# Unread matmuls ahead of the first batch's kv: six of them made to wait for a cast of k

## The chip, the cores and the metric

One core of a Trainium2 chip. The metric is the time of one execution on the device, in microseconds (us), as the median of several; differences here are tenths of a microsecond of 288, so single executions are listed where they matter. The profile's span, from the first to the last instruction, is a different clock: in the runs below the time is the span plus 1.8 to 1.9 us.

## The reference

Linear attention, then layer norm and a two-layer feed-forward, on 8 batches of 8 heads, 576 positions and 64 per head:

```python
kv  = einsum('bhsd,bhse->bhde', k, v)
o   = einsum('bhsd,bhde->bhse', q, kv)
x   = o / sqrt(mean(o*o, -1) + 1e-6) * g_norm          # then heads side by side: (8, 576, 512)
xn  = (x - mean) / sqrt(var + 1e-6) * g_ln
out = x + relu(xn @ w_ch1) @ w_ch2                     # 512 -> 2048 -> 512
```

## The kernel before

Almost all of the time is large matrix products on PE (TensorE). The argument is about the first 17 us, in which batch 0 is loaded, its kv is formed and a first tile is taken to the first large product. All loads of v, q and the weights come through POOL's queue, in this order; k comes as float32 by two other queues and is cast by DVE and ACT:

```python
nc.sync.dma_start(k_f[:, :HP // 2], pairs(k, 0, HP // 2))
nc.scalar.dma_start(k_f[:, HP // 2:], pairs(k, HP // 2, HP))
nc.gpsimd.dma_start(v_p[:, :HP - 1], pairs(v, 0, HP - 1))          # three of four pairs of heads: "v"
nc.gpsimd.dma_start(q_in[0][:64, :, :2], lo(q, 0)[:, :, :2])
nc.gpsimd.dma_start(v_p[:, HP - 1:], pairs(v, HP - 1, HP))
nc.gpsimd.dma_start(q_in[0][:64, :, 2:], lo(q, 0)[:, :, 2:])
load_w1(0)
# ...
nc.vector.tensor_copy(k_p[:, :HP // 2], k_f[:, :HP // 2])
nc.scalar.copy(k_p[:, HP // 2:], k_f[:, HP // 2:])
```

While these run PE has nothing to do, and is kept busy with products of zeros that nobody reads ("fills"). More of them stand between later steps of the start:

```python
def fill(n, p1=None):
    if p1 is None:
        p1 = ps2.tile([128, 512], f32, tag="p2", name="p1")
    for _ in range(n):
        nc.tensor.matmul(p1, lhsT=fill_sb[:, :128], rhs=fill_sb, start=True, stop=True)
    return p1
# ...
fill(18)
# ...
kv_a.mms()            # 54 products of 64x64 for three pairs; waits for k's cast and for v
kv_a.copies()
turn_first(0, ps2, "p2")
kv_a.times_g()
fill(1)
kv_b.mms()            # the fourth pair
# ... o, squares, sums, root, a scaled copy, then the large products
```

## Time and profile before

| | |
|---|---|
| median of three timed runs | 288.02 us (287.99 to 288.05) |
| the profiled run | 290.37 us, span 288.5 us, mean clock 0.993 |
| PE busy | 280.6 us, 97% of the span |
| fills end, then kv starts | 6.93 us, 9.51 us |
| first large product starts | 17.09 us |

In a timeline line the first number is the start, the second the length, and the bracket says how long the engine had been idle and what released it. In a line of windows, the numbers after the length are the busy time of PE, of its weight loads, of DVE, ACT and POOL, each with a count of instructions; then come the granted clock of PE (1.00 is full speed), the share of the DMA engines, and GB/s. The lines of this profile stand in the prediction.

### The profile page before, as it was taken

How to read it: one execution, taken by the hardware profiler on the slowest of the kernel's cores; microseconds unless marked ns; L12 is line 12 of the kernel's file. 1: busy time of each engine (PE TensorE's matmuls, PEld its weight loads, DVE VectorE, ACT ScalarE, POOL GpSimd, SP SyncE). 2: the span in 40 equal slices, each digit the busy share in tenths (PEclk: the TensorE clock that was granted, in tenths of full speed). 3: DMA queues.
4: the chain of work that ended last, by engine and by line, in shares of the span. 5: the costliest groups of instructions: out<-in, count | busy, mean ns of one | idle time of the engine just before them, and what ended most of it. 6: DMA issues, size and time to landing. Idle time of an engine off the chain costs nothing.

```text
span 288.5 us, 5777 instructions
## 1 busy us (share of the span) xinstructions
PE 280.6 (97%) x2302; PEld 159.2 (55%) x2302; DVE 150.4 (52%) x335; ACT 152.9 (53%) x334; POOL 44.2 (15%) x74
## 2 busy tenths in 40 slices
PE   7699999999999999999999999999999999999995
PEld 3479855996569644445444544444444444444444
DVE  5566207946997884675366565762578200220022
ACT  3367754796649733882289248920894076016500
POOL 8432630023025004100620020000000000000000
PEclk9799999999999999999999999999999999999999
DMA  7999999949988989994999897038202610131033
GB/s 207 199 205 204 199 183 190 228 94 172 149 164 131 187 134 176 212 133 97 155 221 190 144 128 163 18 63 173 58 18 60 106 36 0 41 83 24 0 74 73
DMA packets 67442, 36.76 MB, mean 127 GB/s; under 512 B 35536, under 2 KB 62548, under 8 KB 67416
## 3 DMA queue, kind: packets, MB, share of 16 engines
q0 software_dynamic: 28736, 18.29, 44.4%
q1 hardware_dynamic: 38168, 17.39, 31.3%
q10 hardware_dynamic: 512, 0.72, 0.8%
q8 instruction: 18, 0.29, 0.4%
q14 instruction: 8, 0.07, 0.1%
HBM read 36.71 MB, written 9.44 MB: 160 GB/s over the span
## 4 chain that ended last, share of the span: by engine, by line
PE 94%; DMA 3%; ACT 1%; issue 0%; DVE 0%; POOLq 0%
PE p L489 43%; PE p L473 43%; DMA v_in<-in_v_dram 3%; PE o_ps L281 3%; PE kv_ps L254 2%; PE p L206 1%; PE tp L192 1%; ACT m L476 1%; PE og_ps L293 0%; ACT xT_blk L410 0%; PE odd L233 0%; PE tp L408 0%; ACT xT_blk L334 0%; DVE ss L358 0%; PE o_part L566 0%
## 5 line engine op out<-in xcount | busy, mean ns | idle before, releaser
L473 PE MATMUL p<-xT_blk,w_sb 128*128 128x128 bf16 (+2 forms) x1024 | 132.0, 286 | 0.6 <-ACT xT_blk L334 0.3
L489 PE MATMUL p<-w_sb,m 128*128 128x512 bf16 (+2 forms) x608 | 128.2, 368 | 0.0
L476 ACT ACTIVATE m<-p 128x512 bf16<-128x512 f32 x144 | 85.2, 595 | 46.8 <-PE p L473 44.5
L473 PEld LDWEIGHTS <-w_sb 128*128 128x128 bf16 x1024 | 78.6, 98 | 44.7 <-issue 1.3
L489 PEld LDWEIGHTS <-m 128*128 128x128 bf16 x608 | 57.3, 98 | 63.0
L494 DVE SCALAR_TENSOR_TENSOR o_sb<-p,rstd,x_blk 128x512 f32<-128x512 f32 (+2 forms) x38 | 27.2, 720 | 47.7 <-PE p L489 47.5
L287 ACT ACTIVATE sq<-o_ps 128x512 f32<-128x512 f32 x35 | 20.9, 596 | 27.0 <-PE o_ps L281 26.8
L400 ACT ACTIVATE dev<-x_blk,st_blk 128x512 f32<-128x512 f32 x36 | 25.7, 714 | 13.1 <-DVE st_blk L386 13.1
L358 DVE TENSOR_REDUCE ss<-sq 128x8 f32<-128x512 f32 x35 | 23.6, 678 | 16.4 <-ACT sq L287 16.4
L392 DVE SCALAR_TENSOR_TENSOR xc<-x_blk,st_blk,g_ln_sb 128x512 bf16<-128x512 f32 x34 | 25.6, 752 | 1.5 <-DVE st_blk L386 0.3
L363 DVE TENSOR_TENSOR y<-o_ps,inv 128x512 f32<-128x512 f32 x33 | 22.8, 692 | 3.1
L382 DVE SCALAR_TENSOR_TENSOR x_blk<-y,g_norm_sb 128x512 f32<-128x512 f32 x33 | 22.8, 692 | 1.1
L375 DVE RECIPROCAL inv<-rms 128x8 f32<-128x8 f32 x36 | 7.2, 201 | 22.9 <-ACT rms L368 22.9
L482 DVE RECIPROCAL rstd<-rstd 128x4 f32<-128x4 f32 x9 | 1.6, 174 | 30.8 <-ACT rstd L481 30.7
L368 ACT ACTIVATE rms<-ss,eps_sb 128x8 f32<-128x8 f32 x36 | 10.6, 295 | 11.6 <-DVE ss L358 11.5
L281 PEld LDWEIGHTS <-qt 128*128 128x128 bf16 (+1 forms) x156 | 10.6, 102 | 6.3 <-issue 0.7
L281 PE MATMUL o_ps<-kv_pack,qt 128*128 128x128 bf16 (+1 forms) x156 | 13.8, 221 | 0.0
L98 POOL COPY gate<-qt 1x1 bf16<-1x1 bf16 x5 | 0.9, 176 | 82.1 <-DMA qt<-q_p 82.1
L206 PE MATMUL p<-fill_sb 128*128 128x512 bf16 x24 | 8.2, 489 | 1.3 <-DVE eps_sb L142 1.3
L259 ACT CAST kv_pack<-kv_ps 64x256 bf16<-64x256 f32 x7 | 2.6, 365 | 11.4 <-PE kv_ps L254 11.4
L400 ACT ACTIVATION_READ_ACCUMULATOR dev<-x_blk,st_blk 128x1 f32 x36 | 6.8, 189 | 0.0
L254 PEld LDWEIGHTS <-k_in 128*64 128x64 bf16 x280 | 4.9, 113 | 2.2 <-issue 2.1
(94 smaller groups left out, 118.2 us busy)
## 6 DMA issues: line engine op xcount, KB each, us to landing
out_dram<-o_sb SPq DMA_DIRECT2D x66, 128.0 KB, 2.4
w_sb<-in_moe_w_ch_dram POOLq DMA_DIRECT2D x7, 512.0 KB, 13.9
q_in<-in_q_dram POOLq DMA_DIRECT2D x7, 320.0 KB, 9.7
k_in<-in_k_dram POOLq DMA_DIRECT2D x7, 320.0 KB, 8.6
v_in<-in_v_dram POOLq DMA_DIRECT2D x7, 320.0 KB, 10.3
q_in<-in_q_dram POOLq DMA_DIRECT2D x8, 256.0 KB, 10.7
k_in<-in_k_dram POOLq DMA_DIRECT2D x7, 256.0 KB, 9.2
v_in<-in_v_dram POOLq DMA_DIRECT2D x7, 256.0 KB, 12.5
```

Of the source, the lines that this page charges most:

```text
L206: nc.tensor.matmul(p1, lhsT=fill_sb[:, :128], rhs=fill_sb, start=True, stop=True)
L281: nc.tensor.matmul(flat[rows, hp * 128:(hp + 1) * 128], lhsT=lhsT_of(hp), rhs=kvp[:, hp, :], start=True, stop=True)
L287: nc.scalar.activation(self.sq_t, self.o_ps, func=AF.Square)
L358: nc.vector.tensor_reduce(self.ss, self.sq_t, axis=AX.X, op=ALU.add)
L363: nc.vector.tensor_mul(self.y_t, self.o_ps, self.inv().to_broadcast([128, H, D]))
L382: nc.vector.scalar_tensor_tensor(x_blk[:, ts].rearrange("p (h d) -> p h d", h=H), in0=self.y_t, scalar=1.0, in1=g_norm_sb.to_broadcast([12 ...
L392: nc.vector.scalar_tensor_tensor(self.xc_t, in0=x_blk[:, self.ts], scalar=st[:, 1, self.ts:self.ts + 1], in1=g_ln_sb, op0=ALU.add, op1=ALU ...
L400: nc.scalar.activation(dev, x_blk[:, ts], func=AF.Square, bias=st[:, 1, ts:ts + 1], accum_out=st[:, 2, ts:ts + 1])
L473: nc.tensor.matmul(p1[:, i, :], lhsT=w1_sb[:, kk, de * 128:(de + 1) * 128], rhs=blk[2][:, kk, sl], start=(kk == 0), stop=(kk == nK - 1))
L476: nc.scalar.activation(m1[:, de0:de0 + per, sl], p1, func=AF.Relu)
L489: nc.tensor.matmul(p2[:, c0:c1], lhsT=m1s[b][:, de, ts * 128:(ts + 1) * 128], rhs=w2_sb[:, de, c0:c1], start=(de == 0), stop=(de == nDe - 1))
L494: nc.vector.scalar_tensor_tensor(o_sb[:, c0:c1], in0=p2[:, c0:c1], scalar=rstds[b][:, ts:ts + 1], in1=blks[b][0][:, ts, c0:c1], op0=ALU.mu ...
```

## The change

In the profile before, the clock of PE falls to half (0.50, from 11.31 us on) after PE has been idle for 2.58 us. The fills are meant to prevent that, and the change lets them reach closer to the arrival of v: fifteen at once, then six that read the cast half of k and so cannot start before it, in place of eighteen at once.

```diff
-    def fill(n, p1=None):
+    def fill(n, p1=None, rhs=fill_sb):
         if p1 is None:
             p1 = ps2.tile([128, 512], f32, tag="p2", name="p1")
         for _ in range(n):
-            nc.tensor.matmul(p1, lhsT=fill_sb[:, :128], rhs=fill_sb, start=True, stop=True)
+            nc.tensor.matmul(p1, lhsT=fill_sb[:, :128], rhs=rhs, start=True, stop=True)
         return p1
@@
-    fill(18)
+    fill(6, fill(15), k_p[:, 0, :512])
```

## The prediction

> **What bounds the kernel now.** I read the page first, then the chain that ended last in order of time, then the timeline of the first 18 us engine by engine, and last the table of windows at 0.1 us for the granted clock.
>
> The page says that PE is the bound nearly everywhere, and that the only hole in its row is at the start, where the clock row has a hole too:
>
> ```profile
> PE 280.6 (97%) x2302; PEld 159.2 (55%) x2302; DVE 150.4 (52%) x335; ACT 152.9 (53%) x334; POOL 44.2 (15%) x74
> PE   7699999999999999999999999999999999999995
> PEclk9799999999999999999999999999999999999999
> ```
>
> A slice is 7.2 us, so the 7 in the clock row lies between 7.2 and 14.4 us. The timeline of PE shows what the change is about, the unread matmuls ("fills") and the wait after them:
>
> ```profile
> 1.34 5.59 PE L206 MATMUL p<-fill_sb 128*128 128x512 bf16 x18 [1.34 <-DVE eps_sb L142]
> 9.51 0.19 PE L233 MATMUL even<-v_in,k_in 64*64 64x64 bf16 x1 [2.58 <-DMA v_in<-in_v_dram]
> ```
>
> Eighteen fills end at 6.93, then PE idles 2.58 us until v lands. Nothing before 9.51 can be won on PE, because the chain that ended last goes through the transfer of v and not through the fills:
>
> ```profile
> 1.25 8.22 DMA v_in<-in_v_dram
> ...
> 11.59 0.60 PE o_part L566 x4
> 12.19 0.57 PE tp L192 x16
> 12.76 0.54 PE og_ps L293 x4
> 13.30 1.28 PE p L206 x3
> 14.58 0.35 PE o_ps L281 x4
> ```
>
> From 11.59 the chain is PE's for 5 us. Three fills there take 1.28 us, 0.43 each. In the timeline of the weight loads the first fills also follow one another at 0.43 us (2.60, 3.03, 3.45), but the nine from 4.61 on take 1.83 us, 0.216 each. So PE runs at half speed in this stretch, and the windows say from when to when (columns: window, length, busy time of PE, PEld, DVE, ACT, POOL, then the granted clock):
>
> ```profile
> 11.20:11.30 0.10, 0.10 (x16) 0.10 (x13) 0.09 (x1) 0.10 (x1) 0.04 (x2) 1.00 1.30 213
> 11.30:11.40 0.10, 0.10 (x14) 0.10 (x7) 0.10 (x1) 0.10 (x1) 0.10 (x1) 0.53 1.35 225
> ...
> 14.60:14.70 0.10, 0.10 (x4) 0.10 (x2) 0.10 (x2) 0.00 (x0) 0.10 (x1) 0.50 1.12 184
> 14.70:14.80 0.10, 0.10 (x3) 0.04 (x1) 0.07 (x2) 0.00 (x0) 0.10 (x1) 0.90 1.18 195
> ```
>
> A mean of 0.53 puts the fall at 11.31, a mean of 0.90 the return at 14.72: 3.41 us at half clock.
>
> [...] 3.41 us from fall to return, and the fall is 6.8 us, two windows, after the fills speed up (between 4.31 and 4.61). So I place the boundaries at about 1.07, 4.48, 7.89, 11.31 and 14.72. [...] a gap of 2.58 us was followed by the fall. [...] the fills show 0.43 and 0.216.
>
> **The change part by part.** *Removed:* three of the eighteen first fills. They were warm ones, so the first group ends 3 x 0.216 = 0.65 earlier, near 6.28. *Added:* six fills that read the first 512 columns of the cast k, which lie in the half that DVE casts:
>
> ```profile
> 5.90 0.76 DVE L540 CAST k_in<-k_f 128x1152 bf16<-128x1152 f32 x1 [1.34 <-DMA k_f<-in_k_dram]
> ```
>
> That cast ends at 6.66; with the 0.04 that the chain shows as issue after a wait, the six start near 6.70. They have no wait among themselves, so the last starts 5 x 0.216 later, at 7.78, and with 0.39 for one it ends near 8.17. *Moved:* nothing else; the built program has six more rows on PE (three loads, three matmuls) and the same counts on the other engines, POOL's and SP's order untouched.
>
> By itself the addition costs nothing: k's first product waits for v at 9.47, 1.3 us after the last added fill. It buys nothing by itself either. What it does is to split one idle stretch of 2.58 into about 0.42 (6.28 to 6.70) and 1.34 (8.17 to 9.51), together 1.76. In the window 7.89 to 11.31, after which the clock fell, idle time goes from 1.62 to 1.34; over the two windows since the speed-up from 2.58 to 1.76 of 6.83, that is from 38% to 26%. The window 4.48 to 7.89 had 0.96 idle and did not bring a fall at its end. If one window decides, the threshold lies somewhere between 0.96 and 1.62 and the new 1.34 is about in the middle; if two decide, the move is large. Hence a bit over even odds that the fall at 11.31 goes away.
>
> **What the half clock costs.** If PE alone set the pace, 3.41 us at half speed would cost 1.7. It does not: DVE and ACT take their share. I redo the stretch at full clock.
> - The copies of kv for the last pair wait for DVE and ACT, busy to 11.57 and 11.52 whatever PE does, so they start near 11.58 instead of 11.61.
> - The first part of o (three matmuls at 0.055 instead of 0.11) then lets the square on ACT start near 11.92 instead of 12.12: 0.20 won. The copy of q's second turn, the sums, the root, the reciprocal and xb follow with the same 0.20, xb ending near 14.56 instead of 14.76.
> - The three fills no longer stand for 1.28 us before the next o: it starts when its q is copied, near 13.2 instead of 14.37, and the square on ACT follows near 13.7 instead of 14.97.
> - Then DVE binds: its sum starts when xb is done, near 14.62 instead of 15.60, takes 0.69, then the root on ACT (0.30 and two gaps of 0.04), so the scaled copy that lets the first large product start begins near 15.7 instead of 16.67. That is 0.95 to 1.0 won.
>
> After that the chain is PE's with short ACT pieces, so an earlier start carries to the end unless a load is late. By the landing records of the trace the last piece of w2 (its last four blocks) lands at 46.10 and is first used near 46.97, by the fifth of the twelve products whose group starts at 46.10 (4 x 0.216 after). Slack 0.87. The other loads have more: the first piece of w1 lands at 14.2 for a start at 17.09, q's upper half at 16.2 for 18.27. So about 0.87 survives, a little more if that transfer moves as well. Sum: 288.02 - 0.87 = 287.15 with the fall gone, 288.0 with it kept.
>
> **The rivals.** (1) *The fall stays.* The added fills give the deciding window only about 0.28 us more[...]. For: the last added fill ends just after the boundary at 7.89. [...] Time 287.95 to 288.1. I give it 0.3. (2) *The fall moves.* PE at full speed has less busy time between 11.31 and 14.72: it would wait for copies, squares and roots, and the fall could come at 14.72, in the dense products, where 3.41 us at half clock cost up to 1.7. Against: five fills of 0.22 stand in that stretch, and the waits I find above sum to under 1 us, less than the 1.62 that brought the fall before. Time 288.3 to 288.9. I give it 0.07. (3) *The fills delay kv.* If k lands late, the six fills push past v. k's cast would have to end 1.3 us later; both transfers were issued first. 0.03, time 288.1 to 288.4. (4) *The boundary is not where this profile has it* in other executions[...]. Then the gain would differ between runs and the median would lie between the two values. The three times before differ by 0.06 only, which speaks against a fall that comes and goes before the change; after it, runs may differ.
>
> **Range and chances.** About 0.6 for 287.0 to 287.3, 0.3 for about 288.0, 0.1 above. The median of that is near 287.25, which I predict. The range 286.9 to 288.15 takes both main outcomes and leaves out the moved fall. A 2% change would be 5.8 us; no part of this argument reaches it, since even all half-clock time is worth 1.7. Faster by over 2% 0.005, within 2% 0.985, slower by over 2% 0.01.
>
> **What would show it right or wrong.** In the timeline of PE: fifteen fills ending near 6.3, six from 6.7 to 8.2, and kv still at 9.5 behind the transfer of v. If the six start elsewhere, the reading of the cast is wrong; if kv starts later, rival 3. In the clock row: no 7 in the second slice, and 1.00 in all windows from 11 to 15. If 0.50 still stands there, rival 1; if it stands between 14.7 and 18.2, rival 2. In the timeline: the three fills that took 1.49 us from 13.09 take some 0.8, the first scaled copy starts near 15.7, the first large product near 16.1 instead of 17.09. If the first large product is early by about 0.95 and the end is not early by 0.8 or more, a load has taken the rest: PE would then show an idle stretch on a piece of w2 near 46. The prediction is wrong if the clock stays whole and the time does not fall by at least 0.5.

Windows and boundaries are my estimate: the trace has the clock change at 4.48, 11.31 and 14.72, which is 6.83 and 3.41 us apart, and 1.07 and 7.89 are set at steps of 3.41 from there. Rival 1: its 0.3 stands as a guess.

## The result, and the profile after

288.09 us (six runs: 288.06, 288.10, 288.08, 287.93, 289.33, 288.34) against 288.03 (six runs, 287.93 to 288.10) for the kernel before. The ratio is 1.001, with a 95% interval of 0.9993 to 1.0026. A ratio here is the mean time of one kernel's fast runs over that of the other's of the same rounds, so not quite the ratio of the two medians. I had forecast a gain of 0.77; there is none.

Yet the profile after looks as I had foretold for the good case. The page of the changed kernel, span 286.2 us, has no hole in the clock row:

```profile
PE 279.0 (97%) x2279; PEld 158.8 (55%) x2305; DVE 151.0 (53%) x335; ACT 152.9 (53%) x334; POOL 44.0 (15%) x74
PE   8999999999999999999999999999999999999995
PEclk9999999999999999999999999999999999999999
```

(PE's count of 2279 is short of the 2302 before because some matmul records are missing; the loads, 2305 for 2302, are the three more that were foretold.) Its timeline of PE has the two groups of fills, and kv:

```profile
1.34 5.40 PE L206 MATMUL p<-fill_sb 128*128 128x512 bf16 x15 [1.34 <-DVE eps_sb L142]
6.70 1.46 PE L206 MATMUL p<-k_in,fill_sb 128*128 128x512 bf16 x6
8.23 0.19 PE L233 MATMUL even<-v_in,k_in 64*64 64x64 bf16 x1
```

The six run from 6.70 to 8.16, as worked out. (The fifteen do not: they end at 6.74, not near 6.28, and leave no idle stretch before the six.) But kv starts at 8.23, not at 9.51: v came 1.3 us earlier than in the profile before, which the change cannot have done. And the chain that ended last no longer goes through v, but through the first piece of w1:

```profile
4.08 10.63 DMA w_sb<-in_moe_w_ch_dram
14.71 0.05 issue
14.75 1.17 PE p L473 x16
```

So the first large product started at 14.75 instead of 17.09, the span is 2.3 us shorter, and the time is the same as that of the timed runs before. The sum works out only if the profiled execution before was not like the timed ones. It took 290.37 us, and they took 288.02; 288.06 is what the profiled execution after took.

The landing of v tells where the first 1.3 us came from. In these traces a transfer lands in sixteen shares (the page counts 16 DMA engines), and each has its time:

```text
profile of            15 of 16 shares of v landed by    the last one
before                8.37                              9.47
after                 8.18                              8.19
```

One share of sixteen came 1.1 us late, and kv waited for it: it started at 9.51, 0.04 after the last share and 1.14 after the fifteenth (in the profile after at 8.23, 0.04 after the last). It was not v alone: the last shares of the next five transfers of the same queue came 0.5 to 1.2 us after their fifteenth in this profile. Why they were late no view shows.

### The profile page after: what moved, and what is told of

Same layout as the page of the kernel before. It is cut to its first block, busy times and chain, and to the rows that moved or that the text cites. A ratio compares the mean times of both kernels' runs of the same rounds, so it can differ in the third digit from the quotient of the medians.

```text
span 286.2 us, 5757 instructions
## 1 busy us (share of the span) xinstructions
PE 279.0 (97%) x2279; PEld 158.8 (55%) x2305; DVE 151.0 (53%) x335; ACT 152.9 (53%) x334; POOL 44.0 (15%) x74
## 3 DMA queue, kind: packets, MB, share of 16 engines
HBM read 36.71 MB, written 9.44 MB: 161 GB/s over the span
## 4 chain that ended last, share of the span: by engine, by line
PE 91%; DMA 4%; ACT 1%; issue 1%; POOL 1%; DVE 0%; POOLq 0%
PE p L489 43%; PE p L473 43%; DMA w_sb<-in_moe_w_ch_dram 4%; PE o_ps L281 3%; PE kv_ps L254 2%; ACT m L476 1%; ACT xT_blk L410 0%; PE tp L408 0%; POOL v_in L131 0%; POOL q_in L132 0%; DVE ss L358 0%; POOL q_in L134 0%; PE tp L192 0%; ACT sq L287 0%; PE tp L179 0%
## 5 line engine op out<-in xcount | busy, mean ns | idle before, releaser
L489 PE MATMUL p<-w_sb,m 128*128 128x512 bf16 (+2 forms) x592 | 126.4, 368 | 1.2 <-issue 0.5
L281 PEld LDWEIGHTS <-qt 128*128 128x128 bf16 (+1 forms) x156 | 10.4, 101 | 6.0 <-issue 0.4
L206 PE MATMUL p<-fill_sb 128*128 128x512 bf16 x20 | 7.2, 499 | 1.4 <-DVE eps_sb L142 1.3
```

The source lines that it names most:

```text
L281: nc.tensor.matmul(flat[rows, hp * 128:(hp + 1) * 128], lhsT=lhsT_of(hp), rhs=kvp[:, hp, :], start=True, stop=True)
L489: nc.tensor.matmul(p2[:, c0:c1], lhsT=m1s[b][:, de, ts * 128:(ts + 1) * 128], rhs=w2_sb[:, de, c0:c1], start=(de == 0), stop=(de == nDe - 1))
```

## The experiments

**Theory A:** the profile before was of an unusual execution. v was late by chance, this made PE's idle stretch long enough for the clock to fall, and the timed executions had neither, so there was nothing to win. **Theory B**, its rival: the half clock is in the usual executions too, and what the change won was lost again, for instance to the first piece of w1. Later two more questions came up. **C:** can fills overshoot the arrival of v and delay kv? **D or E:** does the change do what it is meant for, where v is late, or nothing even then?

Twelve kernels ran, in three calls; each call ran on one chip, with eleven runs of the kernel before beside them (medians 288.00, 288.06 and 288.06). All gave correct results.

### Both kernels unchanged, once more

> The kernel before, unchanged, once more with a profile. Theory A (the profile that I predicted from was of an unusual execution: it took 290.37 us with a span of 288.5, while the timed ones took 288.0; its v landed at 9.47 instead of some 8.25, and the half clock was a follow-up of that): most executions have a span of 286.1 to 286.3, v releases the first product of kv at about 8.3, PE idles some 1.3 us before it and not 2.58, and no clock of 0.50 stands between 8 and 16 us. Theory B (the half clock is in the usual execution too, and what the change won by removing it was lost again, for instance to the first piece of w1, for which PE waited 0.38 us at 14.75 in the changed kernel): the profile shows 0.50 for about 3.4 us somewhere between 8 and 16 us although the span is about 286.2.

> The changed kernel, unchanged, once more. Both theories: 288.0 to 288.1 and a ratio of 1.000 within 0.0015. Theory A says that the 289.33 among its first six runs was an execution with a late v and not a property of the change, so if such runs appear they appear in the kernel before as well.

Measured: before 287.98 us (287.86 to 288.12, five runs, every clock 1.0), after 288.12 (287.96 to 288.27, clocks 0.998 to 1.0), ratio of after to the eleven runs of before 1.0003 (0.9992 to 1.0015). The second profile of the kernel before, taken in the execution of 287.86 us, has in its page and its timeline of PE:

```profile
PEclk9999999999999999999999999999999999999999
```

```profile
1.34 6.72 PE L206 MATMUL p<-fill_sb 128*128 128x512 bf16 x18 [1.34 <-DVE eps_sb L142]
8.14 0.19 PE L233 MATMUL even<-v_in,k_in 64*64 64x64 bf16 x1
...
11.34 0.81 PE L206 MATMUL p<-fill_sb 128*128 128x512 bf16 x3
...
14.57 1.25 PE L473 MATMUL p<-xT_blk,w_sb 128*128 128x128 bf16 x16 [0.29 <-ACT xT_blk L334]
```

kv starts at 8.14, the three later fills take 0.81 us (they took 1.49 in the timeline of the first profile, at half clock), and the first large product starts at 14.57 without any change to the kernel. In the DMA view (KB, then us from issue to landing) v took 6.8 us here; the first profile of the same kernel had 8.2:

```profile
v_in<-in_v_dram POOLq DMA_DIRECT2D x1, 432.0 KB, 6.8
```

```profile
v_in<-in_v_dram POOLq DMA_DIRECT2D x1, 432.0 KB, 8.2
```

38 timed executions of the kernel before have their clock on record: none is under 0.998, where 3.41 us at half clock in a span of 288 would leave at most 0.994. (In the profile after, the last product ends at 282.74 and the clock falls at 285.30, 0.9 us before the end of the span: that makes its 0.998. I take the other values of 0.997 to 0.999 for the same.) Two of the 38 took longer than 288.4, 288.75 and 289.01, both with a clock of 1.0. The recorded clock does not count half clock ahead of its first rise, though: fill0 below has 5.84 us of it from the start of kv on, and a recorded 0.998. That form of B is excluded by the times, since fill0 took 289.93 to 291.00 us and none of the 38 over 289.01. Theory A holds and B falls.

One thing here was not expected. The fills end at 8.06 in this execution and at 6.93 in the other, though they are the same eighteen. The clock became whole at 6.76 here and at 4.48 there. In the thirteen traces with fills ahead of kv it becomes whole anywhere from 4.06 to 6.99, so the point from which the 3.41 us are counted is different in each execution. With a late rise, the fills take 0.427 us each for longer (0.216 after it). That is what question C asks about.

### Eighteen changed to twenty-four; fifteen alone; none

```diff
-    fill(18)
+    fill(24)        # fill15: fill(15); fill0: the line is taken out
```

> Twenty-four fills at once instead of eighteen, none waiting for k. In the profiles so far the clock becomes whole at 4.2, 5.4, 6.8 or 7.0 us, at a different point in each execution; with w for that point, fills at 0.427 us before it and 0.216 after it, N of them end near 0.494 w + 0.68 + 0.216 N. Theory C (a longer train of fills overshoots the landing of v, near 8.2, in executions whose clock becomes whole late, and then delays kv; this is what the change adds in some executions): 24 fills end between 7.6 (w 3.6) and 9.3 (w 7.0), so kv is delayed by 0 to 1.1 us, on average 0.3 to 0.4; the time is 288.2 to 288.6 with a spread of up to 1 us, and the profile shows PE going from fills to kv with no wait for v. Rival (fills are free up to v whatever their number, since the rest of the start has slack): 288.0 within 0.15.

Measured: 289.12, 288.15, 288.55 and 288.03 us (median 288.35), clocks 0.998 to 1.0. The profile is of the execution of 289.12, whose clock became whole at 6.95:

```profile
1.34 8.10 PE L206 MATMUL p<-fill_sb 128*128 128x512 bf16 x24 [1.34 <-DVE eps_sb L142]
9.38 0.21 PE L233 MATMUL even<-v_in,k_in 64*64 64x64 bf16 x1
```

The last share of v had landed at 8.14. PE went on with fills to 9.44 and started kv at 9.38, 1.24 us late, and the execution is 1.06 us longer than the median of before. So fills do overshoot, and the delay reaches the end. The traces put the end of N fills at 0.494 w + 0.83 + 0.216 N, w being when the clock becomes whole (the 0.68 of the expectation leaves out the last fill's own tail). With w near 7 the twenty-one of the change end at 8.82 (seen in a_late, w 6.97), some 0.6 after v would have landed, and the eighteen of before at 8.17 (b_late, w 6.99), no later than v. Over the thirteen values of w that the traces show, I estimate that the change would delay kv in six, by up to some 0.5 us and by 0.15 to 0.2 in the mean. Its eleven runs have a median of 288.10 where 44 of before have 288.04 (means 288.22 and 288.07), which is the right sign, but the interval above includes no difference, and no trace of the change with v on time and a late w was caught: argued, not shown.

> The first half of the change alone: fifteen fills at once and nothing after them. They end near 5.7 to 7.4, so PE idles 0.8 to 2.5 us before v. Theory A (with v on time the idle stretch is too short for the clock to fall, in nearly all executions): 288.0 within 0.15, clocks of 0.998 and above, an odd execution with the fall at about 289. If the wait of 2.5 us in early executions is enough for the fall, about a third of the executions are 0.7 to 1.1 us longer with a clock near 0.994.

Measured: 287.93, 288.05, 288.14, 288.15, 288.23, with clocks of 0.998 and above, and one of 291.27 with a clock of 0.987. With v on time these fills leave an idle stretch of 0.7 to 2.1 us (estimated: fifteen fills end at 6.08 in a_mid and 7.52 in a_late, and v releases kv near 8.2), and none of the five had the fall, as theory A has it. (By the border found below about half of them should have had it; what that says of the border stands there.) The sixth execution was the profiled one, and shows the accident again: fifteen shares of v landed by 8.55, the last at 9.32.

```profile
1.34 5.33 PE L206 MATMUL p<-fill_sb 128*128 128x512 bf16 x15 [1.34 <-DVE eps_sb L142]
9.36 0.21 PE L233 MATMUL even<-v_in,k_in 64*64 64x64 bf16 x1 [2.68 <-DMA v_in<-in_v_dram]
```

The clock fell at 8.69 and was half for 6.83 us, twice 3.41, to 15.52. A late v and fewer fills together cost 3.2 us.

> No unread matmuls ahead of kv at all. It sizes what half clock costs when v is on time: PE starts kv at 8.2 with half clock and gets the whole one at a boundary between about 10.4 and 14. From my working of the prediction 3.4 us of half clock in this stretch cost about 1.0; here 2.2 to 5.6 us are at half clock, so 288.6 to 289.6, mean about 289.1, all executions above 288.4. If half clock cost nothing here (all hidden behind DVE, ACT and the first piece of w1, which lands at 13.2 to 14.7), 288.0 to 288.2.

(The boundary between 10.4 and 14 is an estimate from the traces up to then: the clock whole first at 7.0 us at the latest, and 3.41 us for a step.)

Measured: 289.93, 291.00, 290.26 and 290.93 us (median 290.59). In the profile, of the first of them, PE starts kv at 8.23 and is at half clock to 14.07 (its products of kv follow at 0.027 us each, against 0.016 at whole clock in the first profile): 5.84 us, for 1.9 us of time (289.93 against 288.06). That is 0.32 us per us, close to the 1.0 for 3.41 us of my working. I expected a mean of 289.1 and the others are longer still; they were not traced. In the traced one, half clock outlasted the 3.41 us from 7.24 to 10.65, in which PE was busy for 2.02 us, with kv's small products and the turns of q. All fills ahead of kv together are worth 2.5 us; three fewer, or three more as in the change, nothing that can be measured with v on time.

### Twelve at once, then the six that wait

```diff
-    fill(6, fill(15), k_p[:, 0, :512])
+    fill(6, fill(12), k_p[:, 0, :512])
```

> As the change, but twelve fills at once ahead of the six that wait for k, eighteen in all as before. The last one ends near 8.0 in executions whose clock becomes whole early (k's cast binds) and no later than in the kernel before in the others, so nothing overshoots v. Theory C: 288.0, as before, and no runs of 288.25 to 288.35 beyond what the kernel before has. Rival (the wait for k or the read of k itself costs): 288.1 to 288.15 like the change.

Measured: 288.03, 287.99, 287.97, 288.45 (median 288.01; ratio to before 0.9999, 0.9986 to 1.0011). It is not above before, as C has it, but four runs with one of 288.45 do not tell it from 288.1. Inconclusive.

### v made late on purpose

To see whether the change does its work at all, v is issued behind other pieces, so that it lands late in every execution. In the pair called "mid" one piece of q is ahead of it, and v lands near 9.2, about as in the accident; in the pair called "late", the small piece of v as well, and v lands at 9.6 to 10.0.

The edit of "mid", made to both kernels (b_mid is the kernel before with it, a_mid the changed one; b_late and a_late likewise):

```diff
-    nc.gpsimd.dma_start(v_p[:, :HP - 1], pairs(v, 0, HP - 1))
-    nc.gpsimd.dma_start(q_in[0][:64, :, :2], lo(q, 0)[:, :, :2])
+    nc.gpsimd.dma_start(q_in[0][:64, :, :3], lo(q, 0)[:, :, :3])
+    nc.gpsimd.dma_start(v_p[:, :HP - 1], pairs(v, 0, HP - 1))
     nc.gpsimd.dma_start(v_p[:, HP - 1:], pairs(v, HP - 1, HP))
-    nc.gpsimd.dma_start(q_in[0][:64, :, 2:], lo(q, 0)[:, :, 2:])
+    nc.gpsimd.dma_start(q_in[0][:64, :, 3:], lo(q, 0)[:, :, 3:])
```

> The kernel before with one piece of q (three rows of blocks, 192 KB) issued ahead of the large transfer of v, so that v lands near 9.3, as late as in the two executions whose last sixteenth of v came late (9.3 and 9.5). Late v alone costs about 1.1: 289.1 in executions whose clock stays whole. Eighteen fills end between 6.3 and 8.0, so PE idles 1.3 to 3.0 us. Theory D (the change does do what it is meant for, only where v is late): in some executions, those whose clock became whole early, the clock falls (mean clock 0.994 or less) and they take 290.0 to 290.4; the others 289.1. Theory E (the change does nothing even then): the same mix as a_mid.

> The changed kernel with the same v near 9.3. Its last fill ends near 8.0 to 8.7, so PE idles at most 1.3 us. Theory D: no fall in any execution (all clocks 0.997 and above), all near 289.1, so 0.2 to 0.6 below b_mid in the mean. Theory E: falls and times as in b_mid.

Measured: before with this v, 290.15 (clock 0.993), 289.00, 288.90, 289.09, 289.10 (0.998 and above). The change with this v, 289.02, 288.97, 288.94, 288.99, 289.00 (0.997 and above). The windows differ. This is the one of before, in the execution of 290.15, after which the clock fell (at 11.09), and the next:

```profile
7.68:11.09 3.41, 1.85 (x89) 1.58 (x88) 1.52 (x7) 0.73 (x2) 2.27 (x4) 1.00 1.35 199
11.09:14.50 3.41, 3.12 (x40) 2.10 (x33) 2.52 (x9) 1.92 (x6) 1.33 (x2) 0.50 1.32 203
```

And these are the same ones of the change, where it did not fall:

```profile
7.48:10.89 3.41, 2.27 (x79) 1.53 (x78) 1.46 (x7) 0.52 (x3) 2.18 (x4) 1.00 1.34 199
10.89:14.30 3.41, 3.28 (x62) 2.22 (x64) 2.65 (x9) 2.88 (x8) 1.61 (x3) 1.00 1.33 205
```

PE was busy for 1.85 of 3.41 us in the one and for 2.27 in the other. The fall cost 1.13 us (290.15 against a mean of 289.02 of the other four), close to my 0.95 to 1.0. The two are a fair pair, as their windows start at nearly the same time. Theory D fits: in this pair the added fills made the difference. How often they save that is not shown, as one fall in five against none in five can be chance.

> The kernel before, with the large transfer of v issued after the first piece of q and the small piece of v instead of ahead of them, so that v lands about 1 to 1.3 us later in every execution (about 9.3 to 9.5). Theory A: PE idles about 2.5 us after its eighteen first matmuls, as in the profile before; the clock falls to 0.50 for 3.41 us in some or all executions, the time is 289.2 to 290.4[...]. Theory B expects the late v alone, about +1.2, and no more half-clock time than it has already.

> The changed kernel with the same late v. Theory A: six of its matmuls run from 6.7 to 8.2, PE idles about 1.2 us before kv, the clock stays whole, the time is about 289.2, that is 0.3 to 1.0 us less than b_late of the same call. Theory B: the same time as b_late within 0.2 us.

Measured: before 289.37, 289.47, 289.50, 289.49 (clocks 0.999 and above), 290.81 (0.994) and 293.10 (0.982). The change 289.46, 289.42 (0.999), 290.17 and 289.89 (1.0), and 290.62 (0.992). The lateness alone costs 1.4. Both kernels have executions with the fall (that of the change by its clock alone; it was not traced), so for a v this late the change is not enough, and my expectation that it would be 0.3 to 1.0 lower failed: the means are 290.29 and 289.91, the medians the other way round, 289.50 and 289.89. The runs of 290.17 and 289.89 with a whole clock I cannot account for; neither was traced.

```diff
-    fill(6, fill(15), k_p[:, 0, :512])
+    fill(12, fill(15), k_p[:, 0, :512])      # with the late v of b_late and a_late
```

> The changed kernel with v near 9.7 as in a_late, but twelve fills waiting for k instead of six, so that they end between 9.3 and 10.0. Theory D (the idle stretch decides over the clock, and six fills were too few for a v this late): no execution with a clock under 0.997, and 289.4 to 289.7 in all, against up to 290.6 with a clock of 0.992 in a_late. If falls of the clock come all the same, the idle stretch ahead of kv is not what brings them.

Measured: 289.42, 289.40, 289.45, 289.51, 289.51, clocks 0.997 and above. The profile has fills up to kv, and its window after the clock became whole has no idle time at all:

```profile
6.98 2.75 PE L206 MATMUL p<-k_in,fill_sb 128*128 128x512 bf16 x12
9.66 0.21 PE L233 MATMUL even<-v_in,k_in 64*64 64x64 bf16 x1
```

```profile
6.22:9.63 3.41, 3.41 (x16) 1.36 (x14) 1.48 (x6) 1.14 (x1) 2.94 (x4) 1.00 1.27 202
```

With fills up to the arrival of v there was no fall and no spread, as theory D has it: filling the idle stretch ahead of kv goes with the fall's absence. Five executions without one, where two of six (b_late) and one of five (a_late) had it, support this and do not prove it.

### A try at a faster version

```diff
-    nc.gpsimd.dma_start(v_p[:, :HP - 1], pairs(v, 0, HP - 1))
+    nc.gpsimd.dma_start(v_p[:, :2], pairs(v, 0, 2))
+    nc.gpsimd.dma_start(v_p[:, 2:HP - 1], pairs(v, 2, HP - 1))
@@
-    fill(18)
+    fill(12)
```

> A try at a faster version, as v's landing and not the fills sets the start: the kernel before with the large transfer of v cut in two (two pairs of heads, then one) and twelve fills instead of eighteen, so that the products of the first two pairs run while the third is still on its way. They are 36 of 54 products of 0.015 us, so kv of three pairs ends up to 0.5 us earlier, less one more issue on POOL of about 0.6 us, which the full queue may hide. 287.5 to 287.8 if the rest follows, 288.0 if the first piece of w1 (13.2 to 14.7) binds instead, 288.3 or more if the added issue delays q and w1.

Measured: 287.94 us in one execution, with a clock of 1.0, and 288.99, 289.00, 289.01, 290.17 and 292.25 in five with clocks of 0.981 to 0.993. A failure: PE starts kv at 7.48, but with twelve fills and then small products with a gap between them, the clock fell in nearly every execution. The window before the fall:

```profile
6.29:9.70 3.41, 2.10 (x72) 1.53 (x71) 2.16 (x9) 1.49 (x3) 3.22 (x5) 1.00 1.40 195
```

Two things were changed at once, so which of them brought the falls is not told apart. Even with a whole clock it was only 0.1 below before. No version here beats the two kernels.

### The deciding windows together

In the five traces with a fall it came 3.41 us after the clock had become whole (fifteen fills, b_late, v_split) or 6.83 us after (before, b_mid), and it lasted 3.41 us, with fifteen fills 6.83. So I count windows of 3.41 us from the point where the clock became whole. The table has PE's busy time in the window that ended with a fall, or did not, at whole clock. Left out are windows that nothing hangs on: all others at whole clock up to 20 us have 2.57 and more, and stayed.

| trace | window | PE busy | then |
|---|---|---|---|
| fifteen fills, v late by chance | 5.28 to 8.69 | 1.40 | fell |
| b_late | 6.99 to 10.41 | 1.52 | fell |
| before, first profile | 7.89 to 11.31 | 1.80 | fell |
| b_mid | 7.68 to 11.09 | 1.85 | fell |
| v_split | 6.29 to 9.70 | 2.10 | fell |
| a_mid | 7.48 to 10.89 | 2.27 | stayed |
| before, first profile | 4.48 to 7.89 | 2.46 | stayed |
| a_late | 6.97 to 10.38 | 2.47 | stayed |
| before, second profile | 6.76 to 10.18 | 3.29 | stayed |
| after | 5.40 to 8.82 | 3.34 | stayed |

Ten windows, and one border between 2.10 and 2.27 tells them apart. It was drawn after the fact, and it is no rule: the executions that were not traced speak against it. I work out (an estimate) what it would have at each of the thirteen values of w, with kv near 8.2 in fill15, near 9.2 in b_mid and near 9.65 in b_late (late_full took 289.42 with kv at 9.66, the undisturbed runs of b_late 289.37 to 289.50). The border has the clock fall for 7 of 13, for 8 of 13, and for all 13. By their clocks it fell in none of the five of fill15 with v on time, in one of the five of b_mid, in two of the six of b_late.

The windows differ in more than their sums: those of the falls at 1.80 to 2.10 had 0.55 us of fills or less, the one that stayed at 2.27 had 1.06 (those of the falls at 1.40 and 1.52, mostly fills, had 1.39 and 1.18). Whether a fill and a 64x64 product of kv count alike was not tested. It may also be that the traced executions are not like the rest. Of the fourteen kept traces five show a fall, and in before, fill15 and b_mid the traced execution is the only one with a fall that is on record. Whether tracing, or an execution's place in the series, makes a late share or a fall likelier was not tested.

## Why the prediction was wrong

**The step that failed** is the last term of the sum, "288.02 - 0.87 = 287.15 with the fall gone, 288.0 with it kept". The 0.87 is the worth of something that only the profiled execution had; the 288.02 is the time of executions that had it not. The right base for the subtraction was 290.37, the time of the profiled execution itself. The two traces of the same kernel size what was unusual in it: kv started 1.37 later (9.51 against 8.14), and from there the first large product took 1.15 more (7.58 us after kv against 6.43), together 2.52. The two executions took 290.37 and 287.86, 2.51 apart, so all of it reached the end. I took the span of 288.5 and the time of 288.02 to be the same thing within half a microsecond. The span leaves out 1.8 to 1.9 us of the time, so an execution of 288.02 has a span near 286.15, and 288.5 could not have been one of them.

**Rival 4** was close, and I drew the wrong conclusion from its evidence. Three times within 0.06 us do speak against a fall that comes and goes; I should have gone on to ask whether they all had it or all lacked it.

**What bounds the kernel now** and the reading of the chain were right for their execution. That "nothing before 9.51 can be won on PE" is right in kind; the usual number is 8.2.

**The added fills** came out to the hundredth: start at 6.70, end at 8.16 (predicted 8.17). That is because k's cast, done near 6.66 in both profiles, released them. The first fifteen ended at 6.74, not near 6.28, since the clock became whole at 5.40 and not at 4.48; had it been near 7, the six would have started later too, as in a_late (7.36), so the hundredth is partly luck. "By itself the addition costs nothing" holds in the traced execution. In general it needs the clock to become whole early; with w near 7 the fills should outlast the wait for v (argued above), which I had not considered, as I took w from one trace.

**What the half clock costs** was right in mechanism and nearly in size: 0.95 to 1.0 predicted up to the first large product, 1.15 between the traces and 1.13 in b_mid. The cap of 0.87 by the last piece of w2 did not show: that piece landed at 46.10 in the first profile and at 44.19 in the second of the same kernel. Of these 1.91 us, 0.85 is in the fifteenth of its sixteen shares (44.69 and 43.84); presumably its transfer is released by work that had moved too. The other 1.06 is again a last share that was late in the first profile only.

**Whether the fall goes away** I put at a bit over even, with the threshold between 0.96 and 1.62 us idle. Among the traced windows there is such a border (1.14 to 1.31 us idle by the table), and the pair of b_mid and a_mid lies on its two sides, with v nearly as late as in the first profile; as a rule for all executions it fails. Rival 1, that the fall stays, is what the clock of one execution of a_late, 0.992, says. Rival 2 was not seen. Rival 3 may be real in another form, not because k is late but because the clock is: fill24 shows it for twenty-four fills, for the change it is argued.

My test "the prediction is wrong if the clock stays whole and the time does not fall by at least 0.5" named the outcome exactly.

**Left open:** what rule the clock follows; why a last share is late in some executions, and whether the traced ones have it more often than the others; how often (one of the kernel before among the traced, and the untraced 289.01 of before and 289.33 of the change may be such); and whether the change costs what its overshoot should.

## What to carry to other kernels

Compare the time of the profiled execution with the times of the timed ones before reading a microsecond out of its trace: a profile is one execution, and an idle stretch or a slow clock seen in it may not be in the number that is to be improved. Padding work that is to keep the clock up had two ends here: with fifteen fills and a late v (9.32) the clock fell (291.27 us), and twenty-four with a clock that became whole late (6.95) delayed kv by 1.24 us (289.12); with v on time, three fewer or three more than eighteen changed nothing that could be measured.

## What the traces show of the clock and of late shares

- Gaps of PE of 1.90 us (b_late), 2.41 (b_mid) and 2.58 (the first profile) were each followed by half clock, and v_split fell with no gap over 1 us. PE's busy time within one 3.41 us window told falls from none in the traces (2.10 and less fell, 2.27 and more did not), but the clocks of untraced executions do not fit that border.
- Half clock lasted 3.41 or 6.83 us after a fall. With fills ahead of kv the clock was whole first at 4.06 to 6.99 us, though the fills always start near 1.34. One window mostly of small products did not restore it: with fifteen fills, the window from 8.69 to 12.11 had PE busy for 2.75 us at half clock and the clock stayed half, while one with 2.72 us, all of it fills (a_mid, 0.65 to 4.06), was followed by whole clock. Of the 2.75 us, transposes ran for 0.71 and the 64x64 products of kv for 1.90 (the products overlap in part); whether the kind of product made the difference was not tested.
- The stretch before the first change of the clock on record is shown as 1.00. In the first profile the windows have 1.00 up to 4.48 us, while the fills follow one another at 0.43 us, twice the 0.216 that they take from there on.
- The last share of a transfer was late by 1.10 us for v in the first profile and by 0.77 in the one with fifteen fills, against 0.01 in others, and by 1.51 for the first piece of w1 in the profile after.
